# Sketched attention and a gated FFN on one core: small products moved out of the dummies' PSUM bank, a query set computed in column tiles, and a planner's figures

## Chip, core and metric

The kernel runs on one core of a Trainium2 chip. The time is device microseconds of one execution. The kernel before took 115.51 us (median of three runs, 114.19 to 116.99). A core has TensorE (PE; its weight loads are listed as PEld), VectorE (DVE), ScalarE (ACT), GpSimd (POOL) and SyncE (SP), which here issues most of the transfers. Each engine works through its own instructions in the order in which the program lists them. Products of TensorE go to PSUM, which has 8 banks of 512 fp32 columns on 128 partitions.

## What is computed

```python
q, k, v: (4, 4, 1088, 32)          # batch, head, token, dim
def phi(x):                        # 64 features from two 8-row sketches
    a = einsum('rd,bhsd->bhsr', S1, x); b = einsum('rd,bhsd->bhsr', S2, x)
    return einsum('bhsi,bhsj->bhsij', a, b).reshape(..., 64)
kv  = einsum('bhsf,bhsd->bhfd', phi(k), v)
z   = sum(phi(k), axis=2)
num = einsum('bhsf,bhfd->bhsd', phi(q), kv)
den = einsum('bhsf,bhf->bhs', phi(q), z) + 1e-06
x   = (num / den) as 4352 tokens of 128
out = (relu(x @ w_gate) * (x @ w_val)) @ w_out      # 128 -> 1536 -> 128
```

Inputs and outputs are fp32. The FFN's products run in fp16, and so do those of the feature products; the sketches and denominators are fp32.

## The kernel before, in words

**A planner orders everything.** The kernel describes its work as a list of operations (`P.add(engine, name, duration, function, after, take, drop)`), each with an assumed duration and the operations that it follows. `Plan.run` simulates the engines with these durations, picks on each engine among the operations that are ready the one with the earliest due time, and hands out PSUM banks: an operation that *takes* a `Lease` gets a free bank (or two neighbouring ones), and the bank is free again after the operations that *drop* it. The functions are then called in the order of the planned starts, and this fixes each engine's order in the program. Nothing of the plan's times is in the program: at run time an engine goes on as soon as the semaphores of an instruction are there. The assumed durations (constants beside each `P.add`, and the helpers `dve`, `act`, `pool`, `sk32`, `pe16`) and the times at which inputs are assumed to have landed (`LAND`) thus set the order and nothing else. `T0`, `U` and `LAG` give the FFN's operations their due times.

**Dummies.** Before the first FFN product the loop at the end looks for planned gaps in TensorE's work. `warm(n)` fills them with n products of a 128x128 matrix of zeros (L319), counted at 0.107 us each in the first part (before `WARM`) and 0.056 us behind it. They write columns 0 to 127 of bank 7 (`W_BANK`), and nobody reads them. That bank also has the product of S1 and S2 with the identity (`st_ps`, L324, columns 384 on; read by `make_wS` on ScalarE, L334, and by `make_SA` and `make_WB` on VectorE), `ml_ps` (L338, read by the copy to `ml`, L438) and `sx_ps` (L342, read by `make_L`, L361). The planner may lease bank 7 from 13.0 on.

**Batch 0's start.** k and q arrive in parts. The key side (class `K`): transposes (L489), sketch (L496, 64x32 weights, 16 instructions), transposes back (L507), z (L522), zs (L530: z masked with `ml`), w (L536, from zs and `L`), wc (L541, on ScalarE), the feature products kphi (L549), kv (L562), bd (L569). The casts of v are on ScalarE (L555).

The query side (class `Q`) is cut into sets. The first set of batch 0 (tokens x 0 to 2) goes a way of its own: sketch products of whole 128-column blocks of q as weights (`sk_tok`, L679), evacuated by ScalarE (`t2_tok`, L686), `aT` (L725, L729), denominators (`cx`, L733), `mul_ps` (bw, L742), `red` (L754), `rec` (L759), `rdx` (L762), `rdT` (L767, L772) and the division at the end (`x_div`, L879). The second set of batch 0 (x 2 to 8) uses the same `sk_tok` and `t2_tok`, with `c_tok` (L692) for the denominators: 12 instructions of L679 with 64 columns and 12 of L692 with 32, each with 128x128 fp32 weights; `c_tok` alone waits for wc. All later sets use `sk1` (L701, 64x32 weights: 16 instructions with up to 256 columns), `sk2` (L708, 128x32 weights: 8 instructions), two transposes on VectorE (`t2`, L715, and `t2c`, L721), and have bw and an (L748, L779) on GpSimd. Class `G` then forms the query features (L838), transposes them (L850, evacuated by L857), multiplies by bd (`num`, L865) and writes `xT`.

**FFN** (class `F`): 102 units of 512 columns: `g` (L930) and `v` (L941), ReLU on ScalarE (L935), the product ht on VectorE (L950) or, for each sixth unit, on GpSimd (L946, L954), and `o` (L961) accumulated over the units of a token group, evacuated by L969 and stored (L978). Weights are cast to fp16 on ScalarE (L407), from buffers that batches 2 and 3 use later: SP loads these batches (L210, L276, L216) after the last cast.

Of the kernel before, what the change touches and what calls it, by code (L numbers as in the profile page):

```python
# [12 lines left out]
ACTF = mybir.ActivationFunctionType  # L13
# [133 lines left out]
def kernel(  # L147
# [12 lines left out]
    nc = tc.nc  # L160

    B, H, S, D = q.shape
    R = S1.shape[0]
# [7 lines left out]
    KX = NX + 1  # L171
# [10 lines left out]
    PS = psum.tile([128, 8, 512], FP32, name="ps")  # L182
# [5 lines left out]
    s16 = sb([2 * R, D], FP32, "s16")  # L188
# [58 lines left out]
    W3 = DF // 3  # L247
# [5 lines left out]
    v2 = v32[2].rearrange("p h c -> p (h c)")  # L253
# [28 lines left out]
    id16 = sb([2 * R, 2 * R], FP32, "id16")  # L282
# [26 lines left out]
    sel = sb([2 * R, 16, R], FP32, "sel")  # L309
    nc.vector.tensor_copy(out=sel, in_=id16[:, None, 0:R].to_broadcast([2 * R, 16, R]))  # L310
    selh = sb([H, 4, H, R], FP32, "selh")
# [3 lines left out]
    W_BANK = 7  # L315
# [3 lines left out]
            nc.tensor.matmul(PS[:, W_BANK, 0:128], zero, zero, start=True, stop=True)  # L319

    warm(27)
    st_ps = PS[:, W_BANK, 384:384 + 2 * R]
    for h in range(H):
        nc.tensor.matmul(st_ps[32 * h:32 * h + 32], s16, id16, start=True, stop=True,  # L324
                         skip_group_check=True)
    wS = sb([128, 2, 2, R], FP32, "wS")
    ml_ps = PS[:, W_BANK, 320:320 + H]
    sx_ps = PS[:, W_BANK, 256:256 + D]

    s_t = st_ps.rearrange("p (w i) -> p w i", i=R)  # L330

# [3 lines left out]
                                 scale=maskp[:, i:i + 1])  # L335

    def make_ml():
        nc.tensor.matmul(ml_ps, selh.rearrange("f r h i -> f (r h i)"), id16[0:H, 0:H],  # L338
                         start=True, stop=True)

    def make_sx():
        nc.tensor.matmul(sx_ps, sel.rearrange("f a i -> f (a i)"), s16, start=True, stop=True)  # L342

    SA = sb([128, 4, H, R], FP32, "SA")
    WB = sb([128, 2, H, R], FP32, "WB")
# [12 lines left out]

    def make_L():
        for h in range(H):  # L360
            nc.scalar.activation(out=L[:, h], in_=sx_ps, func=ACTF.Copy, scale=ml[:, h:h + 1])  # L361


    PE0, WARM = 4.2, 6.0
    P = Plan({"PE": PE0, "DVE": 3.3, "ACT": 4.2, "POOL": 3.8, "SP": 3.4, "DMA": 0.0}, range(7))
    P.banks[W_BANK] = 13.0
    T0, U, SLACK = 11.0, 0.74, 0.25
    D1 = 0.0
    DVE_PT = range(3, 10)
# [7 lines left out]
    def dve(cols):  # L377
        return cols / 960.0 + 0.085

    def act(cols):  # L380
        return cols / 1200.0 + 0.045

    def pool(cols):
        return cols * 0.00188 + 0.07

    LAND = {"k0a": 3.6, "S": 3.9, "k0b": 4.3, "q0a": 4.7, "v0": 6.4, "q0b": 7.6,
            "wg0": 8.3, "wv0": 9.0, "wg1": 9.7, "wv1": 10.4, "wo0": 11.1, "wg2": 11.8,
            "wv2": 12.5, "wo1": 13.2, "wo2": 13.9,
            "k1": 15.4, "q1": 16.9, "v1": 18.7, "k2": 20.1, "q2": 21.5, "v2": 23.3,
            "k3": 24.7, "q3": 26.1, "v3": 28.0}  # L390
    land = {n: P.landed(n, t) for n, t in LAND.items()}

    def bank(l, i=0):
        return PS[:, l.banks[i]]

    ws_op = P.add("ACT", "wS", 0.2, make_wS, [land["S"]], rec=0.13)
    sa_op = P.add("DVE", "SA", 0.22, make_SA, [land["S"]], rec=0.07)
    wb_op = P.add("DVE", "WB", 0.15, make_WB, [land["S"]], rec=0.07)

# [9 lines left out]
            (nc.vector if eng == "DVE" else nc.gpsimd).tensor_copy(out=o, in_=wst[w][i])  # L409

    for n, e in CAST.items():
        wcast[n] = P.add(e, n, {"ACT": act(W3), "DVE": dve(W3), "POOL": pool(W3)}[e],
                         lambda n=n, e=e: cast("gvo".index(n[1]), int(n[2]), e), [land[n]],
                         rec={"ACT": 0.13, "DVE": 0.07, "POOL": 0.0}[e])

    class K:


        def __init__(self, b, prev):
# [13 lines left out]
            self.sks.append(P.add("PE", f"ksk {b}", sk32(KX * 32), self.sk, t1 + [ws_op],  # L433
                                  take=[la]))
            if prev is None and b == 0:
                m = P.add("PE", "mlp", 0.2, make_ml, self.sks)
                K.ml_op = P.add("DVE", "ml", 0.1,
                                lambda: nc.vector.tensor_copy(out=ml, in_=ml_ps), [m], rec=0.07)  # L438
                sx = P.add("PE", "sx", 0.2, make_sx, self.sks)
                K.l_op = P.add("ACT", "L", 0.7, make_L, [sx, K.ml_op], rec=0.13)  # L440
            for lo, hi in parts:
                self.t2s.append(P.add("DVE", f"kt2 {b} {lo}", dve((hi - lo) * 64),
                                      lambda lo=lo, hi=hi: self.t2(lo, hi),
                                      self.sks + (prev.uses if prev else []), drop=[la], rec=0.07))
            lz = Lease()
            self.lz = lz
            self.z_op = P.add("PE", f"z {b}", 0.31 if b else 0.5, self.z, self.t2s, take=[lz])
            self.zc_op = P.add("DVE", f"zc {b}", 0.12, self.zc, [self.z_op, K.ml_op], drop=[lz], rec=0.07)
            lw = Lease()
            self.lw = lw  # L450
# [7 lines left out]
            for n, (lo, hi) in enumerate(cut):  # L458
# [11 lines left out]
                else:  # L470
                    phis.append(P.add("POOL", f"kphi {b} {lo}", pool(cols),
                                      lambda lo=lo, hi=hi: self.phi(nc.gpsimd, lo, hi), dep))
            vc = [P.add("ACT", f"vc {b} {h}", act(2 * KX * D), lambda h=h: self.vc(h),
                        [land[f"v{b}"]], rec=0.13) for h in range(2)]
            lm = Lease()
            self.lm = lm
# [106 lines left out]
    rdx = sb([128, 2, H, D], FP32, "rdx")  # L583
    rdT = sb([128, QA], FP32, "rdT")

    class Q:

        def __init__(self, b, x0, n, i, ks, qt1, old):  # L590
            self.b, self.x0, self.n, self.ks = b, x0, n, ks
            i = i % NS
            self.ab, self.c, self.an = q_ab[i], q_c[i], q_an[i]
            self.dn, self.rd, self.bw = q_dn[i], q_rd[i], bw[i]
            first = b == 0 and x0 == 0
            self.first = first
            early = b == 0
            name = f"{b},{x0}"
            cols = n * 32
            wcs = [kk.wc_op for kk in ks]  # L600
            if early:
                la, lc = Lease(), Lease()
                self.la, self.lc = la, lc
                s1 = [P.add("PE", f"qsk {name} {x}", 0.4, lambda x=x: self.sk_tok(x, x + 2),
                            qt1 + [wb_op], take=[la]) for x in range(0, n, 2)]
                t2 = P.add("ACT", f"qt2 {name}", act(2 * cols), self.t2_tok, s1 + old, drop=[la],
                           rec=0.13)
                if first:
                    la.left += n
                if first:  # L610
                    lt = Lease()
                    self.lt = lt
                    at = P.add("PE", f"qaT {name}", 0.45, self.aT, qt1 + [sa_op], take=[lt])
                    ate = P.add("ACT", f"qaTe {name}", act(256), self.aTe, [at], drop=[lt],
                                rec=0.13)
                    s2 = [P.add("PE", f"qc {name}", 0.45, self.cx, [ate, ks[0].zc_op], take=[lc])]
                else:
                    s2 = [P.add("PE", f"qc {name} {x}", 0.27, lambda x=x: self.c_tok(x, x + 2),
                                qt1 + wcs, take=[lc]) for x in range(0, n, 2)]
                o1 = P.add("DVE", f"bw {name}", dve(cols) + 0.03, self.mul_ps, s2 + [t2] + old,  # L620
                           drop=[lc], rec=0.09)
                e, eng = "DVE", nc.vector

                def small(c):
                    return dve(c) + 0.03
            else:
                la = Lease(2)
                self.la = la
                s1 = P.add("PE", f"qsk {name}", sk32(cols, 2, 1) if b is not None else 0.58,
                           lambda: (self.sk1(), self.sk2()), qt1 + wcs, take=[la])  # L630
                t2 = P.add("DVE", f"qt2 {name}", dve(2 * cols), self.t2, [s1] + old, drop=[la],
                           rec=0.07)
                t2c = P.add("DVE", f"qt2c {name}", dve(cols), self.t2c, [s1] + old, drop=[la],
                            rec=0.07)
                e, eng = "POOL", nc.gpsimd

                def small(c):
                    return 0.0018 * c + 0.25

                o1 = P.add(e, f"bw {name}", small(n * H * R), lambda: self.mul(eng),  # L640
                           [t2, t2c] + old, rec=0.07)
            x = n * H
            o2 = P.add("DVE", f"dn {name}", x * (R + 1) / 960.0 + 0.06, self.red, [o1] + old,
                       rec=0.07)
            o3 = P.add("DVE", f"rd {name}", 0.07 + x * 0.0063, self.rec, [o2] + old, rec=0.07)
            if first:

                rx = P.add("ACT", f"rdx {name}", act(256), self.rdx, [o3], rec=0.13)
                lr = Lease()
                self.lr = lr  # L650
                rt = P.add("PE", f"rdT {name}", 0.45, self.rdT, [rx], take=[lr])
                self.rdc = P.add("ACT", f"rdTe {name}", act(256), self.rdTe, [rt], drop=[lr],
                                 rec=0.13)
                self.o4 = t2
            else:
                self.o4 = P.add(e, f"an {name}", small(x * R), lambda: self.div(eng), [o3] + old,
                                rec=0.07)
            self.t2_op = t2
            self.last = []
# [24 lines left out]
        def t2_tok(self):  # L684
# [1 line left out]
            nc.scalar.copy(  # L686
                out=self.ab[:, :, 0:n].rearrange("p w x h f -> p x w (h f)"),
                in_=bank(self.la)[:, 0:n * 64].rearrange("p (x w f) -> p x w f", w=2, f=32))

        def c_tok(self, lo, hi):  # L690
            for x in range(lo, hi):
                nc.tensor.matmul(  # L692
                    bank(self.lc)[:, x * 32:(x + 1) * 32], self.block(x), self.ks[0].wct,
                    start=True, stop=True, skip_group_check=True)

        def sk1(self):
            for p in range(2):
# [409 lines left out]
```

## Time and profile before

| | |
|---|---|
| median of three runs | 115.51 us (114.19 to 116.99) |
| the profiled execution: its time, its span | 113.56 us, 111.8 us |
| mean clock granted to TensorE | 0.946 |
| busy, share of the span: PE, DVE, ACT, POOL | 93%, 76%, 78%, 51% |
| first FFN product (L930) | starts at 20.90 us |
| FFN, most of its time: L930, L941, L961 in the chain that ended last | 18%, 17%, 18% |
| HBM read and written | 9.14 and 2.23 MB |

The span is from the first to the last instruction. A busy TensorE isn't TensorE at its peak: products are pipelined, and their ends are modelled. The chain that ended last is followed back from the last instruction, at each step to what released it or to the instruction before it on its engine. A wait for several semaphores is put down to the one that came last. The granted clock is a share of full speed. All times count from the span's start.

### The profile page before, as it was taken

The page shows a single profiled execution, that of the slowest core. Times are in us where ns is not written, and L with a number is a line of the kernel's source. Part 1 is how long each engine was busy: PE and PEld are TensorE (multiplying, and loading weights), DVE is VectorE, ACT ScalarE, POOL GpSimd, SP SyncE. Part 2 cuts the span into 40 slices and gives each one's busy share as a digit, 9 for nine tenths or more (in the row PEclk, how much of TensorE's full clock was granted, in tenths as well). Part 3 has the DMA queues.
Part 4 walks back from the last instruction along what each step waited for, and adds up shares of the span by engine and source line. Part 5 has one row for each costly group of instructions (what it writes and reads, how often), then busy time and mean ns, then how long its engine had stood idle before and what let it go on. Part 6 is the DMA issues. An engine that isn't in the chain of part 4 may idle for free.

```text
span 111.8 us, 3090 instructions
## 1 busy us (share of the span) xinstructions
PE 104.4 (93%) x1167; PEld 73.6 (66%) x1167; DVE 84.9 (76%) x179; ACT 86.8 (78%) x175; POOL 56.8 (51%) x57
## 2 busy tenths in 40 slices
PE   6895999999999999999999999999999999999950
PEld 6655998967585765655676657466756756667920
DVE  5567504399999999999899595988786696976950
ACT  4337572599799999967996979399789988998930
POOL 4055000647969854795589159829944214272100
PEclk9999555699999999999999999999999999999996
DMA  3999997007899620130013002200310310030041
GB/s 82 308 307 405 412 397 150 10 3 221 283 297 332 134 49 0 28 72 0 0 29 70 0 0 55 45 3 3 76 23 0 70 32 0 16 78 6 5 92 47
DMA packets 9951, 11.57 MB, mean 104 GB/s; under 512 B 1232, under 2 KB 7632, under 8 KB 9936
## 3 DMA queue, kind: packets, MB, share of 16 engines
q1 hardware_dynamic: 9520, 11.01, 34.1%
q10 hardware_dynamic: 416, 0.36, 1.4%
q8 instruction: 9, 0.15, 0.5%
q14 instruction: 6, 0.05, 0.2%
HBM read 9.14 MB, written 2.23 MB: 102 GB/s over the span
## 4 chain that ended last, share of the span: by engine, by line
PE 73%; ACT 11%; DMA 6%; issue 2%; SPq 2%; DVE 1%; POOL 1%; ACTq 0%
PE ps L930 18%; PE ps L961 18%; PE ps L941 17%; DMA v<-in_v_dram 5%; ACT g_sb L935 4%; PE ps L850 3%; PE ps L319 3%; PE ps L679 2%; PE ps L692 2%; PE ps L865 2%; PE ps L562 2%; ACT v L555 2%; DMA out_dram<-o_sb 2%; PE ps L701 1%; ACT qpt L857 1%
## 5 line engine op out<-in xcount | busy, mean ns | idle before, releaser
L950 DVE TENSOR_TENSOR ht<-g_sb,ps 128x512 f16<-128x512 f16 x86 | 55.9, 679 | 12.2 <-ACT g_sb L935 9.0
L935 ACT ACTIVATE g_sb<-ps 128x512 f16<-128x512 f32 x102 | 57.9, 614 | 8.9 <-PE ps L930 7.6
L961 PEld LDWEIGHTS <-ht 128*128 128x128 f16 x408 | 29.8, 98 | 15.1 <-POOL ht L954 2.2
L930 PE MATMUL ps<-xT,wg 128*128 128x512 f16 (+1 forms) x120 | 39.4, 353 | 0.0
L961 PE MATMUL ps<-wo,ht 128*128 128x128 f16 x408 | 38.4, 219 | 0.5 <-DVE ht L950 0.4
L941 PE MATMUL ps<-xT,wv 128*128 128x512 f16 (+1 forms) x120 | 38.8, 348 | 0.0
L954 POOL TENSOR_TENSOR ht<-g_sb,v_sb 128x512 f16<-128x512 f16 x16 | 18.6, 1165 | 23.5 <-ACT v_sb L946 23.5
L838 POOL TENSOR_TENSOR qqp<-qan,qab 128x1024 f16<-128x1024 f32 (+1 forms) x9 | 15.8, 1758 | 11.1 <-DVE qan L779 10.8
L549 POOL TENSOR_TENSOR kp<-kab 128x512 f16<-128x512 f32 (+1 forms) x15 | 17.0, 1159 | 7.5 <-DVE kab L507 7.5
L930 PEld LDWEIGHTS <-wg 128*128 128x128 f16 x120 | 13.3, 115 | 4.5 <-issue 3.6
L941 PEld LDWEIGHTS <-wv 128*128 128x128 f16 x120 | 13.1, 116 | 3.0 <-issue 0.6
L319 PE MATMUL ps<-zero 128*128 128x128 f16 x63 | 6.9, 287 | 2.9 <-ACT L L361 1.3
L946 ACT COPY v_sb<-ps 128x512 f32<-128x512 f32 x16 | 9.5, 594 | 0.0
L319 PEld LDWEIGHTS <-zero 128*128 128x128 f16 x63 | 6.1, 136 | 3.2 <-issue 2.0
L1003 DVE STREAM_TRANSPOSE qT<-q_sb 128x576 f32<-128x576 f32 (+4 forms) x10 | 6.0, 610 | 0.6 <-DMA q_sb<-in_q_dram 0.6
L969 ACT ACTIVATE o_sb<-ps 128x512 f32<-128x512 f32 (+1 forms) x10 | 5.3, 533 | 1.3 <-DMA out_dram<-o_sb 1.3
L489 DVE STREAM_TRANSPOSE kT<-k_sb 128x544 f32<-128x544 f32 (+2 forms) x8 | 5.6, 725 | 0.7 <-DMA k_sb<-in_k_dram 0.7
L884 ACT CAST xT<-ps 128x512 f16<-128x512 f32 (+1 forms) x9 | 4.9, 544 | 1.3 <-PE ps L865 0.6
L555 ACT CAST v<-v 128x576 f16<-128x576 f32 x8 | 5.4, 697 | 0.4 <-DMA v<-in_v_dram 0.4
L850 PE MATMUL ps<-ident,qqp 128*128 128x128 f16 x68 | 5.7, 224 | 0.0
L562 PEld LDWEIGHTS <-kp 128*128 128x128 f16 (+1 forms) x72 | 4.4, 108 | 1.0
L742 DVE TENSOR_TENSOR bw<-qab,ps 128x64 f32<-128x64 f32 (+1 forms) x2 | 0.6, 288 | 5.7 <-PE ps L562 5.1
(90 smaller groups left out, 91.2 us busy)
## 6 DMA issues: line engine op xcount, KB each, us to landing
v<-in_v_dram SPq DMA_DIRECT2D x13, 144.0 KB, 5.1
out_dram<-o_sb SPq DMA_DIRECT2D x28, 64.0 KB, 1.8
k_sb<-in_k_dram SPq DMA_DIRECT2D x3, 544.0 KB, 6.3
q_sb<-in_q_dram SPq DMA_DIRECT2D x3, 544.0 KB, 9.6
k_sb<-in_moe_w_out_dram SPq DMA_DIRECT2D x2, 256.0 KB, 4.9
q_sb<-in_q_dram SPq DMA_DIRECT2D x1, 416.0 KB, 4.9
out_dram<-o_sb SPq DMA_DIRECT2D x10, 32.0 KB, 2.8
k_sb<-in_k_dram SPq DMA_DIRECT2D x1, 288.0 KB, 2.8
```

Of the source, the lines that this page charges most:

```text
L319: nc.tensor.matmul(PS[:, W_BANK, 0:128], zero, zero, start=True, stop=True)
L549: eng.tensor_tensor(out=self.kp[:, lo:hi].rearrange("p x g (i a c) -> p (x g i) a c", i=2, a=R), in0=src[:, 0, :, :, None].to_broadcast([1 ...
L555: nc.scalar.copy(out=v16[self.b][:, 2 * h:2 * h + 2], in_=v32[self.b][:, 2 * h:2 * h + 2])
L838: eng.tensor_tensor(out=self.qp[:, lo:hi].rearrange("p x g (i a c) -> p (x g i) a c", i=2, a=R), in0=a_in[:, :, :, None].to_broadcast([128 ...
L850: nc.tensor.transpose(self.tr_out()[:, x, p], self.qp[:, x, p], ident)
L930: nc.tensor.matmul(bank(self.lg)[:, y * W:(y + 1) * W], wblock(wg, j), x, start=True, stop=True, skip_group_check=True)
L935: nc.scalar.activation(out=self.gs, in_=bank(self.lg), func=ACTF.Relu)
L941: nc.tensor.matmul(bank(self.lv)[:, y * W:(y + 1) * W], wblock(wv, j), x, start=True, stop=True, skip_group_check=True)
L946: nc.scalar.copy(out=self.vs, in_=bank(self.lv))
L950: nc.vector.tensor_tensor(out=self.ht, in0=self.gs, in1=bank(self.lv), op=ALU.mult)
L954: nc.gpsimd.tensor_tensor(out=self.ht, in0=self.gs, in1=self.vs, op=ALU.mult)
L961: nc.tensor.matmul(o[:, s], self.ht[:, y * W + s * 128:y * W + (s + 1) * 128], wo[:, j // 4, (j % 4) * DM:(j % 4 + 1) * DM], start=(j == 0 ...
```

## The change

- `st_ps` goes to bank 6 (`S_BANK`), which may be leased from 6.0 on. `ml_ps` and `sx_ps` get leases of their own (`l_ml`, `l_sx`), dropped by the copy to `ml` and by `make_L`. Bank 7 keeps the dummies alone, and may be leased from 11.0.
- The second query set of batch 0 goes the way of the later sets: `sk1`, `sk2`, `t2`, `t2c`, with a lease of two banks, and all of it follows wc. Its bw and an are on VectorE (`SMALL`), as they were. `c_tok` is gone.
- Assumed durations and landing times are changed.

```diff
     warm(27)
-    st_ps = PS[:, W_BANK, 384:384 + 2 * R]
+    S_BANK = 6
+    st_ps = PS[:, S_BANK, 0:2 * R]
...
-    ml_ps = PS[:, W_BANK, 320:320 + H]
-    sx_ps = PS[:, W_BANK, 256:256 + D]
...
-        nc.tensor.matmul(ml_ps, selh.rearrange("f r h i -> f (r h i)"), id16[0:H, 0:H],
+        nc.tensor.matmul(bank(l_ml)[:, 0:H], selh.rearrange("f r h i -> f (r h i)"), id16[0:H, 0:H],
                          start=True, stop=True)
...
-        nc.tensor.matmul(sx_ps, sel.rearrange("f a i -> f (a i)"), s16, start=True, stop=True)
+        nc.tensor.matmul(bank(l_sx)[:, 0:D], sel.rearrange("f a i -> f (a i)"), s16, start=True, stop=True)
...
-    P.banks[W_BANK] = 13.0
+    P.banks[W_BANK] = 11.0
+    P.banks[S_BANK] = 6.0
+    l_ml, l_sx = Lease(), Lease()
...
-    LAND = {"k0a": 3.6, "S": 3.9, "k0b": 4.3, "q0a": 4.7, "v0": 6.4, "q0b": 7.6,
-            "wg0": 8.3, "wv0": 9.0, "wg1": 9.7, "wv1": 10.4, "wo0": 11.1, "wg2": 11.8,
-            "wv2": 12.5, "wo1": 13.2, "wo2": 13.9,
-            "k1": 15.4, "q1": 16.9, "v1": 18.7, "k2": 20.1, "q2": 21.5, "v2": 23.3,
-            "k3": 24.7, "q3": 26.1, "v3": 28.0}
+    LAND = {"k0a": 3.55, "S": 4.3, "k0b": 4.2, "q0a": 5.5, "v0": 7.7, "q0b": 8.5,
+            "wg0": 9.0, "wv0": 9.75, "wg1": 10.4, "wv1": 11.0, "wo0": 11.65, "wg2": 12.25,
+            "wv2": 12.9, "wo1": 13.6, "wo2": 14.2,
+            "k1": 16.0, "q1": 17.2, "v1": 20.0, "k2": 21.5, "q2": 22.5, "v2": 24.5,
+            "k3": 26.0, "q3": 27.5, "v3": 30.0}
...
-            if early:
+            if first:
                 la, lc = Lease(), Lease()
...
-                else:
-                    s2 = [P.add("PE", f"qc {name} {x}", 0.27, lambda x=x: self.c_tok(x, x + 2),
-                                qt1 + wcs, take=[lc]) for x in range(0, n, 2)]
...
             else:
                 la = Lease(2)
...
-                e, eng = "POOL", nc.gpsimd
+                e, eng = SMALL if b == 0 else ("POOL", nc.gpsimd)
 
                 def small(c):
-                    return 0.0018 * c + 0.25
+                    return 0.0018 * c + 0.25 if e == "POOL" else dve(c) + 0.03
```

The other assumed durations that change: wS 0.2 to 0.36, the casts of the weights on ScalarE from `act(W3)` to 0.52, those of v from `act(2 * KX * D)` to 0.58, mlp 0.2 to 0.3, sx 0.2 to 0.25, z of batch 0 0.5 to 0.37, qsk of the first set 0.4 to 0.48, qaT 0.45 to 0.62, rdT 0.45 to 0.52.

More of the change, by code (lines that the diff above doesn't have):

```diff
@@ L360, in make_L @@
         for h in range(H):
-            nc.scalar.activation(out=L[:, h], in_=sx_ps, func=ACTF.Copy, scale=ml[:, h:h + 1])
+            nc.scalar.activation(out=L[:, h], in_=bank(l_sx)[:, 0:D], func=ACTF.Copy, scale=ml[:, h:h + 1])
     PE0, WARM = 4.2, 6.0
     P = Plan({"PE": PE0, "DVE": 3.3, "ACT": 4.2, "POOL": 3.8, "SP": 3.4, "DMA": 0.0}, range(7))
-    P.banks[W_BANK] = 13.0
+    P.banks[W_BANK] = 11.0
+    P.banks[S_BANK] = 6.0
+    l_ml, l_sx = Lease(), Lease()
     T0, U, SLACK = 11.0, 0.74, 0.25
@@ L394, in bank @@
         return PS[:, l.banks[i]]
-    ws_op = P.add("ACT", "wS", 0.2, make_wS, [land["S"]], rec=0.13)
+    ws_op = P.add("ACT", "wS", 0.36, make_wS, [land["S"]], rec=0.13)
     sa_op = P.add("DVE", "SA", 0.22, make_SA, [land["S"]], rec=0.07)
@@ L411 @@
     for n, e in CAST.items():
-        wcast[n] = P.add(e, n, {"ACT": act(W3), "DVE": dve(W3), "POOL": pool(W3)}[e],
+        wcast[n] = P.add(e, n, {"ACT": 0.52, "DVE": dve(W3), "POOL": pool(W3)}[e],
                          lambda n=n, e=e: cast("gvo".index(n[1]), int(n[2]), e), [land[n]],
@@ L435, in __init__ @@
             if prev is None and b == 0:
-                m = P.add("PE", "mlp", 0.2, make_ml, self.sks)
+                m = P.add("PE", "mlp", 0.3, make_ml, self.sks, take=[l_ml])
                 K.ml_op = P.add("DVE", "ml", 0.1,
-                                lambda: nc.vector.tensor_copy(out=ml, in_=ml_ps), [m], rec=0.07)
-                sx = P.add("PE", "sx", 0.2, make_sx, self.sks)
-                K.l_op = P.add("ACT", "L", 0.7, make_L, [sx, K.ml_op], rec=0.13)
+                                lambda: nc.vector.tensor_copy(out=ml, in_=bank(l_ml)[:, 0:H]), [m],
+                                drop=[l_ml], rec=0.07)
+                sx = P.add("PE", "sx", 0.25, make_sx, self.sks, take=[l_sx])
+                K.l_op = P.add("ACT", "L", 0.7, make_L, [sx, K.ml_op], drop=[l_sx], rec=0.13)
             for lo, hi in parts:
@@ L446, in __init__ @@
             self.lz = lz
-            self.z_op = P.add("PE", f"z {b}", 0.31 if b else 0.5, self.z, self.t2s, take=[lz])
+            self.z_op = P.add("PE", f"z {b}", 0.31 if b else 0.37, self.z, self.t2s, take=[lz])
             self.zc_op = P.add("DVE", f"zc {b}", 0.12, self.zc, [self.z_op, K.ml_op], drop=[lz], rec=0.07)
@@ L472, in __init__ @@
                                       lambda lo=lo, hi=hi: self.phi(nc.gpsimd, lo, hi), dep))
-            vc = [P.add("ACT", f"vc {b} {h}", act(2 * KX * D), lambda h=h: self.vc(h),
+            vc = [P.add("ACT", f"vc {b} {h}", 0.58, lambda h=h: self.vc(h),
                         [land[f"v{b}"]], rec=0.13) for h in range(2)]
@@ L584 @@
     rdT = sb([128, QA], FP32, "rdT")
+    SMALL = ("DVE", nc.vector)
     class Q:
@@ L596, in __init__ @@
             self.first = first
-            early = b == 0
             name = f"{b},{x0}"
@@ L600, in __init__ @@
             wcs = [kk.wc_op for kk in ks]
[L601 removed]
+            if first:
                 la, lc = Lease(), Lease()
                 self.la, self.lc = la, lc
[L604 removed]
+                s1 = [P.add("PE", f"qsk {name} {x}", 0.48, lambda x=x: self.sk_tok(x, x + 2),
                             qt1 + [wb_op], take=[la]) for x in range(0, n, 2)]
@@ L607, in __init__ @@
                            rec=0.13)
[L608 to L616, printed above, removed]
-                else:
-                    s2 = [P.add("PE", f"qc {name} {x}", 0.27, lambda x=x: self.c_tok(x, x + 2),
-                                qt1 + wcs, take=[lc]) for x in range(0, n, 2)]
+                la.left += n
+                lt = Lease()
+                self.lt = lt
+                at = P.add("PE", f"qaT {name}", 0.62, self.aT, qt1 + [sa_op], take=[lt])
+                ate = P.add("ACT", f"qaTe {name}", act(256), self.aTe, [at], drop=[lt], rec=0.13)
+                s2 = [P.add("PE", f"qc {name}", 0.45, self.cx, [ate, ks[0].zc_op], take=[lc])]
                 o1 = P.add("DVE", f"bw {name}", dve(cols) + 0.03, self.mul_ps, s2 + [t2] + old,
@@ L622, in __init__ @@
                 e, eng = "DVE", nc.vector
-                def small(c):
-                    return dve(c) + 0.03
             else:
@@ L650, in __init__ @@
                 self.lr = lr
-                rt = P.add("PE", f"rdT {name}", 0.45, self.rdT, [rx], take=[lr])
+                rt = P.add("PE", f"rdT {name}", 0.52, self.rdT, [rx], take=[lr])
                 self.rdc = P.add("ACT", f"rdTe {name}", act(256), self.rdTe, [rt], drop=[lr],
@@ L688, in t2_tok @@
                 in_=bank(self.la)[:, 0:n * 64].rearrange("p (x w f) -> p x w f", w=2, f=32))
[L690 to L694, printed above, removed]
         def sk1(self):
```

## Prediction

> **What bounds the kernel now.** I read the slices of the span first, for the engine that is full and for its clock.
>
> ```profile
> PE   6895999999999999999999999999999999999950
> PEclk9999555699999999999999999999999999999996
> ```
>
> TensorE is busy nearly to the end, so it is the bound; but from the fifth slice (11.2 us) to the eighth (22.4 us) its clock is at half. Short windows place the fall and the rise, and what precedes the fall (columns: length; busy time and instruction count of PE, PEld, DVE, ACT, POOL; clock; DMA share; GB/s).
>
> ```profile
> 8.50:9.00 0.50, 0.00 (x0) 0.00 (x1) 0.47 (x2) 0.50 (x2) 0.50 (x2) 1.00 1.06 406
> 9.00:9.50 0.50, 0.00 (x0) 0.00 (x0) 0.50 (x3) 0.50 (x5) 0.50 (x1) 1.00 1.06 410
> ...
> 11.00:11.05 0.05, 0.05 (x6) 0.05 (x2) 0.03 (x1) 0.00 (x0) 0.00 (x0) 0.65 1.27 492
> ...
> 21.25:21.30 0.05, 0.05 (x3) 0.02 (x2) 0.00 (x0) 0.00 (x0) 0.05 (x1) 0.95 0.00 0
> ```
>
> TensorE does nothing between 8.47 and 9.77 us; at 11.02 the clock halves, and it comes back at 21.25. The list of waits names the holders.
>
> ```profile
> PE ps L319 <- ACT L L361: 1.3, 1, 1.3
> DVE ml L438 <- PE ps L342: 1.1, 1, 1.1
> PE ps L319 <- ACT wS L334: 0.6, 1, 0.6
> ```
>
> L319 is the dummy matmuls. They read nothing but zeros, and yet wait for two ScalarE readers whose only tie to them is that they read columns of the same bank 7. L438 (ml) waits likewise for L342 (sx), which it doesn't use. Last, the chain that ended last, in order of time (start, us, what):
>
> ```profile
> 9.00 0.73 ACT L L361 x4
> ...
> 9.77 0.72 PE ps L319 x10
> 10.49 0.42 PE ps L733 x4
> ...
> 11.79 2.56 PE ps L679 x12
> ...
> 15.20 2.51 PE ps L692 x12
> ...
> 17.82 1.01 PE ps L767 x4
> 18.83 0.53 PE ps L319 x5
> 19.36 0.35 PE ps L865 x2
> 19.72 1.39 PE ps L319 x12
> 21.11 0.36 PE ps L930 x2
> ...
> 49.20 0.59 PE ps L701 x16
> 49.80 0.57 PE ps L708 x8
> ```
>
> The first FFN product (L930) can't start before 20.9 us because TensorE works through the second query set of batch 0 (L679, L692: 5.07 us) ahead of L767, on which that product depends. From there on TensorE is the end's measure: counting the products between 35.3 and 60 us at the chain's prices (0.22 us for 512 columns of L930 or L941 or four of L961, 0.45 for eight of L850, and so on) gives about 24.3 us of work in 24.7. Between 20.9 and 35.3 the same count gives 12.65 in 14.4, so 1.75 us (12%) are lost there, where ScalarE is full and its chain shows. So the end moves with the first L930, less what the FFN's first stretch gives back.
>
> **The change, part by part, against the profiled execution (113.56 us: span 111.8 and 1.76 around it).**
>
> *Banks.* The seven dummies at 4.84 no longer wait for wS, so L496 can start when kT is there (L489 ends 4.94) instead of 5.32: 0.3 us, but the transposes behind it stand in VectorE's order behind one that waits for q (L1003, 5.55), so I count 0 (up to 0.3). ml needs only L338, done by 7.23, not 8.19: VectorE's next two (L515 0.39, L549 0.69) move up by 0.95, and zs (L530), which came after them at 9.30, is then held by z's end (8.47): 8.5 at the latest, 7.4 if the new plan puts z ahead of sx and the query products (the transposes it needs end at 7.1). L733 needs zs and aT (7.34) and has no waiting dummies ahead: about 8.8 instead of 10.33. bw (L742) also needs L686 on ScalarE, behind the casts of v (7.76 to 9.0, held by a transfer that stays as it is) and L (0.73): 9.9 if that order stays, 9.2 if L goes ahead of v. So bw moves from 11.02 to between 9.2 and 9.9.
>
> *First set's tail.* From bw to the end of rdx (13.14) before is 2.12 us of VectorE and ScalarE work: now 11.3 to 12.0. L767 at full clock 0.5 and 0.2 of latency, L772 0.37, L879 0.42: x stands at 12.8 to 13.5. num's other inputs (L850 and L857 after the products of L838; the last kv and bd) keep their distance to bw, as long as TensorE is free: about 12 us. First L930: 12.9 to 13.6.
>
> *Second set by 32-column tiles.* L679 x12 and L692 x12 with ScalarE's L686 (0.48) go. In their place come sixteen instructions as L701 and eight as L708 with 192 columns where the rows have 256: 0.75 x 1.16 = 0.87 us at full clock, 1.75 at half, against 5.07. They need q's transposes (landing about 8.5, two transposes 1.03, so 9.55) and wc, that is L (8.1 to 9.7) and 0.4 for L536 and L541: start 9.6 to 10.2, end at most 11.1, before L767 is ready. That wc is now a condition of all of the set costs nothing while L is early; if L is late, the kv and L850 instructions stand behind it in TensorE's queue. VectorE gains two transposes (0.71 x 0.75 = 0.53 and 0.41 x 0.75 = 0.31) and loses nothing but a little of L742: 0.8 us, where it was idle for 5.1 us in one piece. Cover gone, they would put L879 back by up to 0.5.
>
> *Plan figures.* They do no work, but fix the order and the number of dummies. Dummies too many or too early stand in the queue: before, seventeen took 1.92 us between L767 and the first L930. Bounds for this: 0 and 1.0; no gain, since a dummy has no consumer. I take 0.7, nearer the upper end, since those in the row all lay on the path. With rounding up for hand-overs the first L930 comes at 13.9 (bounds 12.9 and 15.1): 7.0 us earlier.
>
> *What is late next.* Weights are issued until 9.15 and take about 4.9 to land, so until about 14.1; their casts (0.52 each) then pile up at ScalarE just as the FFN starts: between 9.9 and 13.9 there is room for four or five of nine beside rdx, qpt, rdT and wc, where before all but two were done. Two or three more casts in a stretch where ScalarE is full: 1.0 to 1.5 us of ScalarE, less the 0.48 of L686; TensorE feels it in part. Bounds 0 and 1.5, taken 0.6. The loads of batches 2 and 3 wait on SP for the last casts, and move up with them.
>
> Batch 1's transfers don't move. By the DMA view k1 is issued at 9.78 and takes 7.4 (17.2), q1 10.40 and 9.6 (20.0), v1 from 11.04 to 13.2 and some 8.8 (20.9 at the last). Before, they are first used by L489 at 23.33, L1003 at 26.48 and L555 at 26.63, so with margins of 6.1, 6.5 and 5.7 us. Moved up by 7.0 all three are too early, by 0.9, 0.5 and 1.3. Each would hold its engine's queue: VectorE's products ht behind L489 and L1003, ScalarE's g_sb behind L555, and TensorE behind these. The waits overlap, so the bounds are 0 (the plan has v1 at 20.0 now and can put it further back) and 1.3; taken 0.7.
>
> Sum: 113.56 - 7.0 + 0.6 + 0.7 = 107.9 on the profiled execution's scale. The three timed runs (114.19 to 116.99, median 115.51) lie above that execution by 1.95 in the median. If their spread comes from the stretch at half clock, it goes with it (107.9); if not, it stays (109.8). I take the middle, **108.8 us**.
>
> **The clock and the rule against it.** The profile gives one fall, after one idle of 1.3 us and little work, and no rise for ten us in which TensorE was occupied without a break, but with narrow fp32 products whose weight loads (333 ns in L679 and L692) outlast their 64 or 32 columns. It rose after a stretch of L767, dummies and wide products. I read from this that the amount of streaming in a stretch decides; in the new order dummies and the dense tiles fill 7.6 to 11. The Trainium skill (TensorE: Matmul & The Clock Gate, Part 1) gives free-running windows of 3.41 us, and 11.02 to 21.25 is three of these, as the trace agrees; but it also has the clock fall only after a whole idle window, and rise after a busy one, which the 1.3 us of idle and the ten busy us contradict. By that rule the wait that goes away isn't what lowered the clock, which is the first rival.
>
> **Rivals.**
>
> *The clock falls anyway, for part of the way.* For: the fall isn't explained by idleness alone, and small products remain before 11 us. Against: L679 and L692, which kept it down, are gone. L767 and the products by it take 0.7 more, the dummies 0.9 more (half of the 1.92 above), hand-overs 0.3, and the first FFN products run at half clock for some 2 us, losing 1.0: 2.9 more; but an FFN that starts 1.9 later has batch 1 in time (0.7 less). 107.9 + 2.2, and the same allowance of 0.9: about 111.0 us. 0.22.
>
> *The wait comes back elsewhere.* Bank 7 is open to leases from 11.0 in the plan, while dummies still write to it until the first FFN product; a dummy that follows a lease waits for its reader, as L319 did for L361. Then only the second set's 3.3 us at half clock are saved, and up to 2 us lost by FFN work at half clock: 111.3 to 113.3 us. 0.10.
>
> *Slower: the new order costs TensorE slots throughout.* The figures re-sort every instruction to the end, and the order before loses almost nothing after 35 us. If the new one lost over the whole 83 us what the old lost in its first 14 (12%), that is 10.0 us in place of some 2.2: 7.8 us, more than the 5.7 gained. Up to a loss of 9% the change still gains; slower by over 2% of the median needs some 12%: about 118 us. Against: the operations after 35 us and their costs are the same, so their relative order should hardly change. 0.05.
>
> **How the numbers follow.** Forecast 0.63, rivals 0.22, 0.10, 0.05. The forecast's own range begins at 106.3 (8.0 us gained, and the 0.7 of batch 1 given back) and ends at 111.2 (5.8 gained, the 1.5 of the casts given back, and the whole offset of 1.95); the first rival reaches a little over 112. I give 106.0 to 112.3. Within 2% of the median (about what a measurement of this kernel can tell from no change) begins at 113.2: the forecast and nearly all of the first rival are below, half of the second. Faster 0.86, same 0.08, slower 0.06.
>
> **What would show it.** Right: no idle of TensorE behind L361; no waits of L319 on ScalarE; ml right behind L338; PEclk without the four fives, or with one or two; the first L930 between 13 and 15 us; 24 tile instructions of about 0.9 us before it; the stretch from the first L930 to the last L961 of about 87 us, as before (20.9 to 107.9). Wrong: fives from 11 us on again (first rival), L319 waiting for a lease's reader (second), PE slots lost after 30 us (third), or VectorE and ScalarE waiting for batch 1's transfers for more than 1.3 us (the margins).

## The result and the profile after

The changed kernel takes 108.05 us (median of four runs, 107.28 to 108.85) against 116.22 (four runs, 114.19 to 116.99): a ratio of 0.9408, 95% interval 0.9258 to 0.9558. The profiled execution took 108.2 us, its span 106.4 (before 113.56 and 111.8). The forecast was 108.8, range 106.0 to 112.3.

In the slices of the span the three fives and the six of the clock are gone:

```profile
PE   6999989959999999999999999999999999999940
PEclk9999999999999999999999999999999999999996
```

The short windows that showed the idle stretch and the fall of the clock now read (length; busy time and count of PE, PEld, DVE, ACT, POOL; clock; DMA share; GB/s):

```profile
8.50:9.00 0.50, 0.50 (x10) 0.50 (x10) 0.36 (x2) 0.50 (x2) 0.50 (x2) 1.00 1.04 397
...
11.00:11.05 0.05, 0.05 (x5) 0.05 (x5) 0.00 (x0) 0.05 (x1) 0.00 (x0) 1.00 0.94 369
...
15.00:15.50 0.50, 0.15 (x2) 0.00 (x0) 0.00 (x0) 0.50 (x3) 0.50 (x1) 1.00 1.05 430
...
21.50:22.00 0.50, 0.00 (x0) 0.00 (x0) 0.50 (x2) 0.50 (x1) 0.00 (x0) 1.00 0.91 181
22.00:22.50 0.50, 0.00 (x0) 0.00 (x0) 0.50 (x1) 0.50 (x2) 0.00 (x0) 1.00 0.55 183
```

TensorE works where it idled before, but has two holes of a new kind behind the start of the FFN, at 15.1 to 15.6 and at 21.5 to 22.8 us. The timeline of the changed kernel gives the first FFN product (L919 now, L930 before) and what stands ahead of it; the second hole is in brackets at L524 (z of batch 1):

```profile
12.49 1.35 PE L319 MATMUL ps<-zero 128*128 128x128 f16 x21
...
13.01 0.36 DVE L868 TENSOR_TENSOR xT<-ps,rdT 128x256 f16<-128x256 f32 x1
...
13.68 0.38 PE L919 MATMUL ps<-xT,wg 128*128 128x256 f16 x2
...
22.77 0.35 PE L524 MATMUL ps<-kab 128*32 128x32 f32 x18 [1.28 <-ACT g_sb L924]
```

The first FFN product starts at 13.68 us, 7.22 earlier; the span is 5.4 shorter; so 1.8 us are given back behind it. The list of waits of the changed kernel says to whom:

```profile
ACT wv L408 <- DMA v<-in_moe_w_val_dram: 1.0, 1, 1.0
PE ps L319 <- DVE maskkv L295: 1.0, 1, 1.0
...
DVE qT L992 <- DMA q_sb<-in_q_dram: 1.0, 1, 1.0
```

L319's only wait left is that for its zeros at the start. The other two are transfers that weren't waited for before: a weight that is cast at 14.45 us, ahead of the first ReLUs on ScalarE, and q of batch 1, for whose transposes VectorE waits until 20.59 us with the transposes back of k of batch 1 (L509) queued behind, on which z depends. The profile puts z's wait down to a ReLU of ScalarE that ends at 22.70 us, 0.07 behind these transposes, so both engines hold it about equally. The chain that ended last (start, us, what) now runs through transfers until 17.58 us and then mostly through ScalarE to z (transfers make 17% of the span, 6% before):

```profile
9.90 7.68 DMA k_sb<-in_k_dram
17.60 0.76 DVE kT L491
...
22.20 0.51 ACT g_sb L924
...
22.77 0.35 PE ps L524 x15
```

### The profile page after: what moved, and what is told of

It is laid out like the page before. It is cut to its first block, busy times and chain, and to the rows that moved or that the text cites. A ratio compares the mean times of both kernels' runs of the same rounds, so it can differ in the third digit from the quotient of the medians.

```text
span 106.4 us, 3113 instructions
## 1 busy us (share of the span) xinstructions
PE 99.4 (93%) x1179; PEld 67.4 (63%) x1179; DVE 85.0 (80%) x181; ACT 85.7 (81%) x174; POOL 56.9 (53%) x57
## 4 chain that ended last, share of the span: by engine, by line
PE 72%; DMA 17%; ACT 5%; SPq 1%; issue 1%; DVE 1%
PE ps L919 20%; PE ps L950 19%; PE ps L930 19%; DMA k_sb<-in_k_dram 10%; DMA k_sb<-in_moe_w_val_dram 5%; PE ps L839 3%; PE ps L854 2%; PE ps L690 2%; ACT g_sb L924 2%; PE ps L697 2%; DMA out_dram<-o_sb 2%; PE ps L564 1%; PE ps L498 1%; ACT qpt L846 1%; ACT o_sb L958 1%
## 5 line engine op out<-in xcount | busy, mean ns | idle before, releaser
L919 PE MATMUL ps<-xT,wg 128*128 128x512 f16 (+1 forms) x120 | 39.0, 351 | 0.1
L930 PE MATMUL ps<-xT,wv 128*128 128x512 f16 (+1 forms) x120 | 38.6, 347 | 0.0
L919 PEld LDWEIGHTS <-wg 128*128 128x128 f16 x120 | 13.2, 114 | 4.3 <-issue 3.3
L930 PEld LDWEIGHTS <-wv 128*128 128x128 f16 x120 | 13.1, 114 | 2.1
L319 PE MATMUL ps<-zero 128*128 128x128 f16 x75 | 6.9, 261 | 1.0 <-DVE maskkv L295 1.0
L319 PEld LDWEIGHTS <-zero 128*128 128x128 f16 x75 | 6.0, 121 | 1.2 <-DVE maskkv L295 1.0
L839 PEld LDWEIGHTS <-qqp 128*128 128x128 f16 x68 | 4.4, 98 | 1.0 <-issue 0.6
L564 PEld LDWEIGHTS <-kp 128*128 128x128 f16 (+1 forms) x72 | 3.8, 98 | 1.4 <-issue 0.5
```

Of the source, the lines that this page charges most:

```text
L839: nc.tensor.transpose(self.tr_out()[:, x, p], self.qp[:, x, p], ident)
L919: nc.tensor.matmul(bank(self.lg)[:, y * W:(y + 1) * W], wblock(wg, j), x, start=True, stop=True, skip_group_check=True)
L930: nc.tensor.matmul(bank(self.lv)[:, y * W:(y + 1) * W], wblock(wv, j), x, start=True, stop=True, skip_group_check=True)
```

## The experiments

A number behind a label is the median of its runs in us, with their span of values.

### Which part carries it

Four kernels, with the change's three parts taken singly or in pairs.

**e1_banks**: the kernel before with the bank part alone.

```diff
-    st_ps = PS[:, W_BANK, 384:384 + 2 * R]
+    S_BANK = 6
+    st_ps = PS[:, S_BANK, 0:2 * R]
...
+    P.banks[S_BANK] = 6.0
+    l_ml, l_sx = Lease(), Lease()
```
and the leases of ml_ps and sx_ps as in the change.

> The kernel before with the bank part of the change alone (st_ps in bank 6, leases for ml_ps and sx_ps; the second set still by L679 and L692; old figures). Theory (the amount of streaming in a stretch sets the clock, and the narrow fp32 products keep it low): the idle of 1.3 us behind L goes, zs and bw move up by about 1 us, but the clock still halves somewhere between 11 and 15 us, and the first FFN product comes at 17.5 to 19.5 us: 111 to 114 us. Rival (the idle stretch alone lowered the clock): full clock throughout, the 9 us at half clock shrink by 4.5, first FFN product at 15 to 16.5 us: 108.5 to 110.5 us.

109.32 (109.0, 109.64, 108.17 and once 114.66); ratio 0.9507, interval 0.9154 to 0.986. Its timeline:

```profile
10.44 1.50 PE L680 MATMUL ps<-WB,qT 128*128 128x64 f32 x12
...
12.24 1.48 PE L693 MATMUL ps<-wc,qT 128*128 128x32 f32 x12
...
15.43 0.38 PE L931 MATMUL ps<-xT,wg 128*128 128x256 f16 x2
```

In this execution the theory fell: the narrow fp32 products of the second set run at full clock (1.50 us for twelve against 2.77) and don't lower it. The rival's numbers came, or nearly so (108.17), in three runs of four. The fourth, 114.66, left no profile, but its mean granted clock is on record: 0.929, against 0.990 to 0.998 in the other three. So it had a long stretch at half clock, and what lowered the clock there isn't shown.

**e2_tiles**: the tiles alone; the diff is the change's in class `Q`, with banks and figures as before.

> The kernel before with the second query set by tiles alone (banks shared with the dummies as before, old figures). Theory: the stall behind L stays and the clock halves at about the same time as before; the 24 tile instructions take 1.75 us instead of 5.07, and the denser work after them brings the clock back one or two windows sooner: first FFN product at 15.5 to 18 us, 109.5 to 112.5 us. Rival (the idle alone counts): the clock halves all the same; no difference in the number. What tells them apart is how long the half clock lasts: under 7 us by the theory, 10 us by a rival in which it must first see a stretch without any idle.

113.01 (112.88, 113.14, 114.98, 110.58). The profiled execution is instructive, for its clock row is 9 in all 40 slices and its products say otherwise:

```profile
4.84 0.90 PE L319 MATMUL ps<-zero 128*128 128x128 f16 x7 [0.56 <-ACT wS L334]
...
7.80 1.22 PE L712 MATMUL ps<-qT,SA 128*128 128x256 f32 x2
...
13.21 0.89 PE L688 MATMUL ps<-qT,wS 64*32 64x192 f32 x16
...
18.31 0.38 PE L917 MATMUL ps<-xT,wg 128*128 128x256 f16 x2
```

Seven dummies in 0.90 us, against 0.55 before, and 1.22 us for the two instructions that take 0.70 in the profiles of before and after: this execution ran at half clock from its first products, at 1 us, to about 16 us. So where the records hold no change yet, the row reads full speed, whatever the clock is. The half clock lasted some 15 us, longer than either side expected, and it wasn't the stall behind L that caused it.

**e3_banks_tiles**: the changed kernel with the old figures.

```diff
-    P.banks[W_BANK] = 11.0
+    P.banks[W_BANK] = 13.0
```
with `LAND` and the durations of before.

> The changed kernel with the old durations and landing times: banks and tiles without the figures. Theory: the figures only re-sort a few neighbours; full clock, first FFN product at 13.3 to 14.5 us, 107.5 to 109.5 us. Rival (the figures matter, the old ones put operations ahead of inputs that have not landed): first FFN product after 15 us, over 110 us.

109.27 (108.11 to 110.82); first FFN product at 14.71 us, just outside what the theory gave. The times of e1_banks and e3_banks_tiles are the same, though the tiles brought the first FFN product 0.72 us forward (15.43 to 14.71).

**e4_figures**: the kernel before with the new durations and `LAND`.

> The kernel before with the new durations and landing times alone. Theory: the waits of the dummies, the fall of the clock and L679 and L692 stay; first FFN product at 20 to 22 us, 114 to 117 us. Rival (the new figures carry part of the gain): below 112 us.

115.82 (116.1, 116.86, 115.54 and once 108.36). In the profiled execution the first FFN product comes at 23.88 us, at half clock from the start (L725 takes 1.22 us). The one run of 108.36 left no profile; its mean granted clock is 0.999. It is as fast as the changed kernel with neither banks nor tiles, so the rival's number came once in four.

### Which wait of the dummies

e4 has runs 8 us apart with one and the same program. The kernel before, run 29 times more beside the experiments, comes in two kinds. In 14 executions, of 113.58 to 116.45 us, the mean granted clock is 0.919 to 0.947: a long fall is on record, as in the profile that the prediction worked from (113.56 us, 0.946). In the other 15, of 115.85 to 117.27 us, it is 0.991 to 0.999, which leaves no room for ten recorded microseconds at half clock (they take some 0.045 off the mean). By the profiles of e2 and e4 (1.000 and 0.991) these were most likely at half clock from the start. So the question was which of the two waits decides: that for wS at 4.2 us, or that for L at 8.5.

**f1_st_back**: the changed kernel with st_ps back in the dummies' bank.

```diff
-    st_ps = PS[:, S_BANK, 0:2 * R]
+    st_ps = PS[:, W_BANK, 384:384 + 2 * R]
```

> The changed kernel with st_ps alone back in bank 7, so that the seven dummies at 4.2 us wait for wS again (0.56 us before). Theory A (what lifts the clock at the start is a stretch of TensorE's work without a hole of half a microsecond; with the hole it is chance): some executions run at half clock from 4.8 to 11 us or longer (seen by dummies 0.107 us apart and L714 at 1.2 us, whatever the clock row says), and come out at 111 to 115 us; the others at 107.5 to 109; the spread grows to over 3 us. Theory B (the early wait matters only for its 0.2 us): 107.3 to 109 in all, spread as the changed kernel's 1.6 us.

111.03 (109.52 to 111.59), neither the one nor the other: all six runs are late. Its waits show that the edit does more than I had thought:

```profile
DVE WB L354 <- PE ps L319: 1.0, 1, 1.0
PE ps L319 <- DVE SA L349: 0.9, 1, 0.9
```

In the new order the seven dummies stand between the readers of st_ps: they wait for SA, and WB waits for them. The hole grows to 0.95 us and the sketches of k follow late. The execution ran at half clock from the start to about 16.5 us (L714 takes 1.22 us), and the first FFN product came at 18.86. So this kernel shows what a shared bank costs here, 3 us, but not the hole by itself.

**f2_mlsx_back**: the changed kernel with ml_ps and sx_ps back in bank 7.

```diff
-        nc.tensor.matmul(bank(l_ml)[:, 0:H], selh.rearrange("f r h i -> f (r h i)"), id16[0:H, 0:H],
+        nc.tensor.matmul(ml_ps, selh.rearrange("f r h i -> f (r h i)"), id16[0:H, 0:H],
```
and so for sx_ps.

> The changed kernel with ml_ps and sx_ps alone back in bank 7. In its order L runs from 7.08 to 7.9 us, and the first dummies behind it stand at 7.7, so they would wait 0.2 us and not 1.3. Theory (the new order has taken most of this wait away by itself): 107.3 to 109.3 us, first FFN product at 13.7 to 14.1. Rival (the separate leases of ml and sx carry the gain): over 110 us.

107.72 (107.42 to 108.38), first FFN product at 14.05: in the new order their leases are worth nothing that can be told.

**g1_st_alone**: the kernel before with st_ps alone in bank 6. **g2_mlsx_alone**: the kernel before with the leases of ml_ps and sx_ps alone.

> The kernel before with one thing changed: st_ps in bank 6. ml_ps and sx_ps stay in bank 7, so L still holds the dummies for 1.3 us. Theory A (the hole behind wS, which keeps the first warm-up from lifting the clock or lets it fall later, is what the banks are worth): nearly all that e1_banks gains, 109 to 111.5 us. Theory B, that of the prediction (the idle behind L lowers the clock): the clock still halves at about 11 us, 113.5 to 117 us.

> The kernel before with ml_ps and sx_ps alone in leases of their own; st_ps stays in bank 7, so wS still holds the seven dummies. Theory A: nearly nothing, 113.5 to 117 us. Theory B (the idle behind L): 109 to 111.5 us, full clock past 11 us.

g1_st_alone: 115.11 (114.04 to 115.99), ratio 0.9955, interval 0.9849 to 1.0061, so no change that can be told. Its seven dummies go straight on at 4.21, and the clock is full from about 5 us until L's stall:

```profile
10.51 0.72 PE L319 MATMUL ps<-zero 128*128 128x128 f16 x10 [1.38 <-ACT L L362]
...
12.67 2.77 PE L681 MATMUL ps<-WB,qT 128*128 128x64 f32 x12
```

The clock falls at 11.35 and rises at 21.6, as in the kernel before (11.02 and 21.25). Two of the six executions have a mean granted clock of 0.992 and 0.993 and the longest times, 115.97 and 115.99. g2_mlsx_alone: two runs at 107.82 and 108.44, four at 115.94 to 117.2. The profiled one is the 107.82:

```profile
5.17 0.55 PE L319 MATMUL ps<-zero 128*128 128x128 f16 x7 [0.55 <-ACT wS L333]
...
8.47 0.73 PE L319 MATMUL ps<-zero 128*128 128x128 f16 x10
...
10.03 1.50 PE L680 MATMUL ps<-WB,qT 128*128 128x64 f32 x12
...
15.02 0.38 PE L931 MATMUL ps<-xT,wg 128*128 128x256 f16 x2
```

Here the dummies at 5.17 were at full clock in spite of their hole, L's stall is gone, and nothing lowers the clock any more. With neither tiles nor figures this run is as fast as the changed kernel. Theory A fell with g1, and theory B holds for where the clock falls; but the four long executions, which left no profile, say that B alone doesn't make the kernel fast. Three of them (115.94, 116.11 and 117.2) have a mean granted clock of 0.992 to 0.997, so what separates them is most likely the clock at 5 us, as it was in e2, e4 and f1; this is read from the means and from those profiles, not seen in these runs. The fourth (116.34) has 0.918: a long stretch at half clock is on record there, in a program that has no wait of the dummies for L, and its cause is open.

### What the dummies and the rest of the start are worth

**f3_no_dummies**: the changed kernel without the 41 products with zeros behind 5.5 us.

```diff
-            if o.start < f0 + 0.1 and o.start - at > 0.1:
+            if 0.1 < o.start - at and o.start < 5.5:
```

> The changed kernel without the dummies behind 5.5 us (the 27 and the seven at the start stay): 41 of 75 products with zeros go, nothing that is computed. Theory (the amount of streaming in a stretch holds the clock up): without them TensorE idles some 3 us of the 6 before the first FFN product, the clock falls in some or all executions, and the time is 109.5 to 114 us. Rival (the dense tiles and the real products are enough): clock stays, and the first FFN product, no longer behind 21 dummies, comes 0.3 us earlier: 107 to 108.3 us.

108.49 (107.82 to 109.21). The windows of its clock:

```profile
11.20:11.30 0.10, 0.10 (x8) 0.10 (x8) 0.10 (x2) 0.10 (x1) 0.00 (x0) 1.00 1.56 533
11.30:11.40 0.10, 0.10 (x7) 0.01 (x2) 0.10 (x1) 0.10 (x2) 0.00 (x0) 0.53 1.12 430
...
18.10:18.20 0.10, 0.10 (x3) 0.10 (x2) 0.10 (x1) 0.10 (x1) 0.00 (x0) 0.84 0.92 208
```

The dummies help to hold the clock: without them it is at half from 11.3 to 18.1 us in the profiled execution, behind only 1.2 us of idle. Four of the six executions have a mean granted clock of 0.941 to 0.968 and two 0.992 and 1.000; the changed kernel's four have 0.990 to 1.000. But the first FFN product comes at 14.70, 1.0 late, and the cost is 0.4 us in the median, which the spreads of the two don't separate. The profiled executions differ by 0.2 us (108.39 and 108.2). In f3's the two holes behind the start of the FFN (0.46 and 1.28 us) are gone, so what the FFN loses there at half clock it would have lost to its transfers.

**f4_casts_pool**: three casts of weights on GpSimd.

```diff
-    CAST = {"wg0": "ACT", "wv0": "ACT", "wg1": "ACT", "wv1": "ACT", "wo0": "ACT",
+    CAST = {"wg0": "ACT", "wv0": "ACT", "wg1": "POOL", "wv1": "POOL", "wo0": "POOL",
```

> The changed kernel with three of nine weight casts (wg1, wv1, wo0) on GpSimd, which is idle from 9.7 to 13.7 us. Theory (ScalarE's casts and its waits for their transfers cost TensorE some of the first FFN microseconds): 1.5 us less on ScalarE, the hole of TensorE at 15.0 to 16.0 us closes, 106.7 to 107.8 us. Rival (batch 1's transfers set the end of that stretch): hole closes, but the next, at 21.5 to 22.8, grows by as much: 107.8 to 108.6 us, no difference.

108.2 (107.57 to 109.42): no difference. The number is the rival's, its mechanism isn't: in the profiled execution the first hole stays, with 0.48 us, as a cast still waits 1.2 us for its transfer, and the second is 0.99 us instead of 1.28. There VectorE's transposes back of k alone hold z, behind the same wait for q of batch 1 (0.9 us).

**g3_land**: batch 1 and the last weights put as late in `LAND` as the trace has them.

```diff
-            "wv2": 12.9, "wo1": 13.6, "wo2": 14.2,
-            "k1": 16.0, "q1": 17.2, "v1": 20.0, "k2": 21.5, "q2": 22.5, "v2": 24.5,
+            "wv2": 14.4, "wo1": 14.4, "wo2": 14.5,
+            "k1": 17.6, "q1": 20.6, "v1": 21.0, "k2": 21.5, "q2": 22.5, "v2": 24.5,
```

> The changed kernel with the landing times of batch 1 and of the last weights as its own trace has them (k1 17.6, q1 20.6, v1 21.0, wv2, wo1 and wo2 14.4 to 14.5), no other edit. Theory (VectorE's transposes of q1 are ordered ahead of the transposes back of k1 and wait 1.0 us for their transfer, and TensorE idles 1.3 us behind that): the hole at 21.5 to 22.8 us closes, 106.6 to 107.6 us. Rival (something else is late there as soon as this hole is gone): 107.6 to 108.6 us.

109.9 (108.56 to 111.46): not better, and inconclusive, for the profiled execution (111.46) drew the half clock at the start, with the start's instructions in the same order as in the changed kernel:

```profile
7.20 1.22 PE L714 MATMUL ps<-qT,SA 128*128 128x256 f32 x2
...
18.62 0.38 PE L919 MATMUL ps<-xT,wg 128*128 128x256 f16 x2
```

So a gapless start makes the early full clock likely, not certain. The execution says nothing on the hole at 21.5 us, since with so late a start nothing waits for the transfers of batch 1: from the first product at 18.62 us the rest of the span is 91.1 us, from 13.68 in the changed kernel it is 92.7.

**g4_loads**: k and q of batch 1 issued ahead of the last third of the gate and value weights and of the last two of the output weights.

```diff
     load_wo(0)
+    load_k(nc.sync, 1)
+    nc.sync.dma_start(out=q_sb[1], in_=flat(q, 1))
     load_w(2)
     load_wo(1)
     load_wo(2)
...
-    load_batch(1)
+    for a in range(4):
+        load_v(nc.sync, 1, a)
```
with `LAND` to match (k1 13.4, q1 14.8, the moved weights 15.4 to 17.4).

> The changed kernel with k1 and q1 issued before the last third of the gate and value weights and the last two thirds of the output weights, and landing times to match. Theory (batch 1's arrival sets the stretch behind the first FFN product): the waits for q1 and k1 go, but the weights of units 4 and 5 come 3 us later and hold the FFN at 16 us instead: 107 to 109 us. Rival (the weights have slack): 106 to 107 us.

107.18 (106.19, 106.58, 106.59, 107.76, 109.07, 109.08), ratio 0.9273, interval 0.9164 to 0.9382. In its profiled execution (106.58) the first FFN product comes at 14.05, and the rest of the span is 90.75 us, 2.0 less than in the changed kernel. The wait for q of batch 1 is gone, and so are both holes. k of batch 1 lands at 14.5 us instead of 17.6, and VectorE, which takes it up earlier, waits 0.5 us for it:

```profile
DVE kT L494 <- DMA k_sb<-in_k_dram: 0.5, 1, 0.5
```

A moved weight is waited for by ScalarE for 0.3 us only, so in this execution the weights have slack, as the rival had it; the median lies in the theory's range. Its three fastest runs lie below the fastest of the changed kernel (107.28); the intervals overlap, so it is the better candidate and not a proven one.

## Why the prediction was right, point by point

- **The bound and the lever** (the end moves with the first FFN product, less what the first stretch gives back): right. 7.0 us were forecast for the move and 7.22 came; 1.3 for what is given back, and 1.8 came. The two holes, 1.74 us together, account for it, so the third rival (slots lost to the end) didn't come; nor did the second, as the dummies wait for no lease's reader.
- **The path to it**: zs forecast between 7.4 and 8.5, seen at 7.43 (z went ahead of the query products); bw 9.2 to 9.9, seen 9.65; x ready at 12.8 to 13.5, seen 13.37; dummies on the path 0.7, seen about 0.3 (x ends at 13.37, the product starts at 13.68). The 24 tile instructions take from 9.97 to 10.98, 1.0 us, forecast 0.87.
- **The early wait for wS counted as nothing** beyond 0.3 us: wrong as a cost. The 0.2 us by which L498 moves are indeed nothing, but the hole behind wS most likely takes part in whether the clock is full at 5 to 6 us. With st_ps alone put back the time is 111.03, though a second wait (WB behind the dummies) is in that number.
- **The stall behind L lowers the clock**: borne out in the old order. With it the clock falls at 11.0 and 11.35 us (the kernel before and g1); in the profiled runs of g2 and e1, without it, it doesn't. One further run of each (0.918 and 0.929) has a long fall on record all the same. In the new order L is early, and the leases are worth nothing (f2).
- **Narrow products keep the clock low, and the dense tiles replace them**: half wrong. L680 and L693 at full clock leave it there (e1, g2), so the tiles weren't needed to hold it. At half clock the tiles seem still to shorten the stretch: the first FFN product comes at 18.3 us in e2, at 23.9 in e4, both at half clock from the start; but the two differ in their figures too.
- **Streaming in a stretch decides, not idleness alone**: g3 is the better support, where TensorE is occupied without a hole from 1 us on and the clock stays at half to about 16 us. f3, with a fall behind 1.2 us of idle in the 6 us before, fits as well but can't tell less streaming from more idleness. The Trainium skill (TensorE: Matmul & The Clock Gate, Part 1) has windows of 3.41 us: 11.31 to 18.13 in f3 is two, 11.35 to 21.6 in g1 three, as the trace agrees; the condition of a whole idle window in its table of the two states isn't met in either run, and the measurement decides. The first rival, built on that condition, didn't come.
- **Casts 0.6, batch 1 0.7**: the sum was 0.5 short. The hole at 15 us, 0.46 us, isn't the number of casts (f4, no difference) but one cast that waits 1.0 us for its transfer. The hole at 21.5 is batch 1, and it is the term that was too small: TensorE idles 1.28 us, where 0.7 were taken and 1.3 was the bound. VectorE waits 1.0 us for q of batch 1, for which the margins gave 0.5. g4 removes the hole with the transfers' order.
- **The spread of the runs**: of the two cases that were averaged the first came, but not for its reason. The spread before came most likely from executions at half clock from the start, and not from the stretch behind 11 us, so that it went with the change was in part luck. The changed kernel's median is 0.15 below its profiled execution; before, the medians lay 2 to 3 us above theirs. From 108.8 the allowance of 0.9 falls away, the earlier first FFN product takes off another 0.2, the larger give-back adds 0.5, and the median takes off 0.15: 108.05.

## What to carry to other kernels

A product that nobody reads still takes part in its PSUM bank's order: dummies belong in a bank of their own, or they stall (1.3 and 0.6 us here) at the very gaps they should fill. Where the clock of TensorE is part of the time, price a wait by what the clock does behind it, not by its length, and read the clock from the durations of known products before the first recorded change. Once the front of a pipeline is 7 us faster, look at the transfers that had 6 us of margin: they are the next bound, and their order is a lever.

## What the runs showed that I had not expected

- The clock row is full speed until the first change on record: in e2, f1 and g3 it shows 9 throughout the start, while the two instructions of the product with SA take 1.22 us instead of 0.70.
- The same program comes out 8 to 9 us apart: g2 at 107.82 and 117.2, e4 at 108.36 and 116.86. With 27 dummies in 3 us and a hole behind them the clock is full at 5 us in some executions and not in others. Without a hole it varies as well: the sketch of batch 0's k behind the dummies takes 0.82 us in the changed kernel and 1.21 to 1.23 in f2, f4, g3 and g4, with the same order ahead of it.
- A fall of the clock can cost little: with 6.8 us at half clock f3's profiled execution is 0.2 us longer than the changed kernel's. It loses the time where the changed kernel has its two holes, 1.7 us together, and has none itself.
